# Summing the softmax divisor on four 32-column tiles of TensorE instead of two 64-column tiles (with two smaller edits at the start and the end)

## The chip, the core and the metric

The kernel runs on one core of a Trainium2 chip. The metric is device time in microseconds (us) of one execution. Three runs of the kernel before gave 939.42, 934.87 and 938.68 us, a median of 938.68 us.

## The reference, cut to what matters

```python
# attention: q, k, v are (4, 8, 768, 64), proj is (64, 6)
q_bits = einsum('bhsd,dk->bhsk', q, proj) > 0        # the same for k
mask   = (bucket of q_bits) == (bucket of k_bits)     # bucket = the 6 bits as a number
scores = where(mask, q @ k.T / 8, -1e9)
attn   = exp(scores - max(scores))
attn   = attn / (sum(attn over keys) + 1e-9)
x      = (attn @ v) as (3072, 512)
# feed-forward: w_in is (512, 2048), w_out is (2048, 512)
h  = x @ w_in
g  = h * erf(softplus(h))
out = g @ w_out
```

The change touches the line that divides by the sum over the keys.

## The kernel before, in words

**Attention.** Two heads make a pair: their 64 rows each fill the 128 partitions, and there are 16 pairs. A pair's 768 queries are worked on in two halves of 384, so there are 32 halves, numbered `h`. For each half the 768 keys come as six blocks of 128. `score` (L521) makes a block's scores for both heads on TensorE, `exponential` (L535) turns them into `e` on ScalarE, `sum_keys` (L547) adds the six `e` tiles of 128 keys x 2 heads x 384 queries element by element on VectorE, and `weigh` (L561) multiplies `e` by `v` on TensorE. Once for each pair, `hash_bits` (L358) projects the next pair's q and k.

**The divisor.** `sum_keys` leaves a tile of 128 partitions; the sum over its partitions is done by TensorE. `divisor` (L592) multiplies by a 128x64 matrix of ones, once for each head, so that head 0 lands on PSUM rows 0 to 63 and head 1 on rows 64 to 127, 384 queries each. An f32 product is two matmul instructions here, so a half gives four of them. `keep_divisor` (L604) copies the 128x384 result to SBUF on ScalarE. When both halves of a pair are there, `spread` (L633) writes one row of each head to DRAM with two DMAs on SyncE's queue, `gather` (L637) reads the 1536 numbers back over 128 partitions, `invert` (L645, L648) takes reciprocals on VectorE, `ungather` (L653) and `widen` (L662) bring them back to 64 rows for each head, `normalise` (L670) multiplies on VectorE, and `send` (L676) stores the pair's rows to DRAM. The last pair's share of this is done by `late` inside the feed-forward part.

**The weights.** The host gives the weights as 64-bit floats. `fetch_weights` (L431) loads them in 32 pieces of 512 KB into two buffers; ScalarE and VectorE turn each into f32 (`square_high` to `add_rest`, L445 to L507), between the attention's own work. The first two pieces are loaded on SyncE's queue, behind the second pair's q, k and v; the other 30 on GpSimd's.

**Feed-forward.** 3072 tokens go in six tiles of 512. Both products are done as seven products instead of eight (Winograd's form of Strassen's method): `product` (L1044) makes the seven of the first, `project` (L1184) the seven of the second (M1 to M7), which gather over four steps in seven PSUM banks. After a tile's last step `combine` (L1199, L1215, L1223) adds the banks into the four output blocks on VectorE and stores them. The last step of all uses the order `LAST` (M5 as the last but one, M3 last); M3's block is then added and stored in two halves.

**What sets the order.** Each part lists its operations with an engine, a cost in us, a rank and the operations that it comes after. `arrange` places them greedily in time by these costs and so fixes the order of the instructions on each engine. The costs are only used for that; on the chip each engine runs its list in order and waits for data.

Of the kernel before, what the change touches and what calls it, by code (L numbers as in the profile page):

```python
# [59 lines left out]
ALU = mybir.AluOpType  # L60
# [3 lines left out]
P = 128  # L64
# [16 lines left out]
class Op:  # L81
# [20 lines left out]
    exponential=(3.56, 5.29),  # L102
# [91 lines left out]
def kernel(  # L194
# [206 lines left out]
    def attention():  # L401
        NS = NPAIR * 4
        with (
# [19 lines left out]
            def fetch_weights(n):  # L423
                if n >= len(pieces):
                    return
                queue = nc.sync if n < 2 else nc.gpsimd
                if not WIDE:
                    queue.dma_start(out=pieces[n][0], in_=pieces[n][1])
                else:
                    raws[n] = rawp.tile([P, WP, 2], I32, name="raw", tag="raw")  # L430
                    queue.dma_start(  # L431
                        out=raws[n][:, :, :].rearrange("p c two -> p (c two)"), in_=pieces[n][1]
                    )
# [151 lines left out]

            def divisor(h):

                i, half = divmod(h, 2)
                d = pairs[i]
                z = d["z_ps"] = bank("z_ps")[:, 0:HS]  # L590
                for ab in range(2):
                    nc.tensor.matmul(  # L592
                        out=z[ab * D : ab * D + D, :],
                        lhsT=ones,
                        rhs=d["sum", half][:, ab, :],
                        start=True,
                        stop=True,
                    )
            def keep_divisor(h):
                i, half = divmod(h, 2)  # L600
                d = pairs[i]
                if half == 0:
                    d["z"] = home(i, "z")
                nc.scalar.copy(out=d["z"][:, half * HS : (half + 1) * HS], in_=d.pop("z_ps"))  # L604

            def leave(h):

# [19 lines left out]
            def spread(i):  # L627

                d = pairs[i]
                zd = d["zd"] = dram.tile([2, S], F32, name="zd", tag="zd")  # L630
                d["zc"] = small.tile([P, 2 * S // P], F32, name="zc", tag="zc")
                for ab in range(2):
                    nc.sync.dma_start(out=zd[ab : ab + 1, :], in_=d["z"][ab * D : ab * D + 1, :])  # L633

            def gather(i):
                d = pairs[i]
# [107 lines left out]
            for what, n in order:  # L744
                if what == "score":
                    i = n // 4
                    after = tuple(("weigh_bits", i, ab) for ab in range(2)) + (("copy_bits", i),)
                    for c in range(GC):
                        free = (slots[-3],) if len(slots) >= 3 else ()
                        pe(score, (n, c), 0.82, after + free)  # L750
                        slots.append(("exponential", n, c))
                elif what == "bits":
                    pe(bits_of, (n,), 1.34, (("start_pair", n), slots[-3]))
                    slots.append(("sign_of", n))
                elif what == "divisor":
                    last = 2 * n + 1
                    pe(divisor, (n,), 0.72, (("sum_keys", last, GC - 1), ("keep_divisor", n - 1)))
                else:
                    h = n // 2
                    after = (("exponential", n, GC - 1),)  # L760
                    if n % 2 == 0:
                        after += (("leave", h - 1), ("leave_plain", (h - 1) // 2))
                    pe(weigh, (n,), 2.02, after)
# [21 lines left out]
            for h in range(NH - 1):  # L785
                i = h // 2
                op(
                    keep_divisor,
                    (h,),
                    "ACT",  # L790
                    0.48,
                    (0, 2 * h, -1),
                    (("divisor", h), ("send", i - 1) if i == NPAIR - 1 else ("widen", i - 1)),
                )
# [5 lines left out]
            for i in range(NPAIR):  # L800
# [32 lines left out]
                        )  # L833
                if i == NPAIR - 1:
                    continue
                op(spread, (i,), "SP", 0.8, (0, n, 0), (("keep_divisor", 2 * i + 1),), late=3.0)
                op(gather, (i,), "SP", 0.35, (0, n, 1), (("spread", i),), late=4.5)
                op(invert, (i,), "DVE", 0.4, (0, n + 8, 3), (("gather", i),))
                op(ungather, (i,), "SP", 0.35, (0, n, 2), (("invert", i),), late=3.0)
# [11 lines left out]
            for n in range(len(pieces)):  # L851
                op(
                    fetch_weights,
                    (n,),
                    "SP" if n < 2 else "POOL",
                    1.0,
                    (0, n),
                    (("start_pair", 1), ("fetch_weights", n - 1), ("add_rest", n - 2), ("exponential", max(2 * n - 2, 0), 1)),
                    late=7.0,
                )  # L860
                fetched = ("fetch_weights", n)
                op(square_high, (n,), "ACT", 0.68, (1, n, 0), (fetched, ("mask_bits", n - 1)))
                op(keep_normal, (n,), "ACT", 0.7, (1, n, 1), (("square_high", n),))
                op(move_bits, (n,), "DVE", 1.05, (2, n, 0), (fetched, ("add_rest", n - 1)))
                op(mask_bits, (n,), "DVE", 1.1, (2, n, 1), (("move_bits", n), ("keep_normal", n)), late=1.5)
                op(add_rest, (n,), "DVE", 1.3, (2, n, 2), (("mask_bits", n),))
# [131 lines left out]
    def feed_forward(check, late):  # L998
        again = late is None
        with (  # L1000
# [194 lines left out]
            def combine(t, k):  # L1195

                if k == 0:
# [1 line left out]
                    nc.scalar.copy(out=outs["u"], in_=banks["M1"])  # L1199
                    return  # L1200
                u = outs["u"]
                name, into, one, where, subs = (
                    ("M2", "c", u, (0, 0), (0, 2)),
                    ("M6", "u", u, None, (0, 2)),
                    ("M7", "w", u, None, (0, 2)),
                    ("M4", "c", outs.get("w"), (1, 0), (0, 2)),
                    ("M5", "u", u, None, (0, 2)),
                    ("M5", "w", outs.get("w"), (1, 1), (0, 2)),
                    ("M3", "u", u, (0, 1), (0, 1)),
                    ("M3", "u", u, (0, 1), (1, 2)),  # L1210
                )[k - 1]
                if into == "c" or k == 3:
                    outs[into] = outp.tile([P, 2, TH], F32, name=into, tag=into)
                subs = slice(*subs)
                nc.vector.tensor_tensor(  # L1215
                    out=outs[into][:, subs, :],
                    in0=banks[name][:, subs, :],
                    in1=one[:, subs, :],
                    op=ALU.add,
                )  # L1220
                if where:
                    r0 = t * T + where[0] * TH + subs.start * P
                    nc.sync.dma_start(  # L1223
                        out=out[
                            r0 : r0 + (subs.stop - subs.start) * P,
                            where[1] * TH : (where[1] + 1) * TH,
                        ].rearrange("(s p) d -> p s d", p=P),
                        in_=outs[into][:, subs, :],
                    )

            ops = []
# [2 lines left out]
                ops.append(Op(name, engine, cost, rank, lambda: fn(*args), **more))  # L1234

            ORDER = ("M1", "M2", "M4", "M5", "M6", "M7", "M3")
            LAST = ("M1", "M2", "M4", "M6", "M7", "M5", "M3")
            EMPTIED = dict(M1=0, M2=1, M6=2, M7=3, M4=4, M5=6, M3=8)
            chain = dict(P=None, M=None, X=None)

            def first_ops(p):
# [63 lines left out]
            def between_ops(p, v):  # L1305
# [3 lines left out]
                for k, (fn, engine, cost, after, more) in enumerate(  # L1309
# [8 lines left out]
                    )  # L1318
                ):
                    after += (previous,) if previous else ()  # L1320
                    if again and previous is None:
                        after += tuple(("gate", p - 1, n) for n in range(2))
                    previous = (fn.__name__, p, v)
                    rank = (1, p + PRIORITY[fn.__name__][v], 0)
                    op(previous, engine, cost, rank, fn, me, after=after, **more)
# [48 lines left out]
            def second_ops(p):  # L1374
# [20 lines left out]
                    M7=(S[2],),  # L1395
                    M3=(S[3],),
                )
                for k, name in enumerate(LAST if p == NP - 1 else ORDER):
                    for f in range(4):
                        me = (name, p, f)  # L1400
                        after = needs[name]
# [43 lines left out]
                else:  # L1445
# [9 lines left out]
                        late=5.0,  # L1455
                    )
                if c == NC4 - 1:
                    for k, (name, others) in enumerate(
                        (
                            ("M1", (("combine", t - 1, 8),)),  # L1460
                            ("M2", (0,)),
                            ("M6", (1,)),
                            ("M7", (2,)),
                            ("M4", (3,)),
                            ("M5", (3,)),
                            ("M5", (4, 5)),
                            ("M3", (5,)),
                            ("M3", (7,)),
                        )
                    ):  # L1470
                        after = ((name, p, 1 if k == 7 else 3),) + tuple(
                            ("combine", t, o) if isinstance(o, int) else o for o in others
                        )
                        op(
                            ("combine", t, k),
                            "DVE" if k else "ACT",
                            0.4 if k > 6 else 0.69 if k else 0.58,
                            (0, p, 30 + k),
                            combine,
                            (t, k),  # L1480
# [144 lines left out]
```

## Time and profile before

| what | value |
|---|---|
| runs | 934.87, 938.68, 939.42 us |
| the profiled execution | 939.42 us, of which 937.5 us are the span of the profile |
| TensorE (PE) busy | 920.8 us (98%) |
| VectorE (DVE) busy | 834.6 us (89%) |
| ScalarE (ACT) busy | 776.2 us (83%) |
| DMA read and written | 64.07 MB and 15.93 MB |
| attention | from the start to about 343 us |
| feed-forward | from about 343 us to the end |

PE's busy time counts matmuls whose ends are modelled, so it does not mean that PE is at its peak. PEld is the load of the stationary operand, which may run beside a matmul. "SPq" is SyncE as the issuer of DMAs. In the chain of waits each step is the time from one piece's beginning to that of the next piece that depended on it; it runs from the last instruction back to the first.

### The profile page before, as it was taken

The numbers are of one execution on the slowest core, as the hardware profiler recorded it, in microseconds if no ns is written. First come the engines' busy times: TensorE is split into PE (matmuls) and PEld (weight loads), VectorE is DVE, ScalarE is ACT, GpSimd is POOL, SyncE is SP. The second block draws the span as 40 slices with busy tenths as digits, with TensorE's granted clock in tenths as the row PEclk, the third lists the DMA queues.
The fourth block names the chain that finished last, engine by engine and source line by source line (L and its number), as shares of the span: only waits on it lengthen the run. The fifth ranks groups of instructions, "written<-read, shape, count | busy, mean of one in ns | idle before, by whom it ended". The sixth has DMA issues, their size and how long they took to land.

```text
span 937.5 us, 12887 instructions
## 1 busy us (share of the span) xinstructions
PE 920.8 (98%) x4875; PEld 666.0 (71%) x4875; DVE 834.6 (89%) x1099; ACT 776.2 (83%) x1002; POOL 17.4 (2%) x35
## 2 busy tenths in 40 slices
PE   8999999999999999999999999999999999999996
PEld 3444444444444458888888888888888888888885
DVE  5998999999999987899999989998899789988995
ACT  5888778867888747999997998899989997899891
POOL 0000000000000000000000000000000000000000
PEclk9999999999999999999999999999999999999999
DMA  8355545565664323010222012211221111011211
GB/s 197 97 152 153 132 130 146 136 193 153 170 159 131 97 86 99 15 45 35 68 78 79 34 35 78 79 34 34 79 66 48 34 59 54 34 34 46 68 35 48
DMA packets 59222, 80.91 MB, mean 86 GB/s; under 512 B 33264, under 2 KB 41968, under 8 KB 59152
## 3 DMA queue, kind: packets, MB, share of 16 engines
q1 hardware_dynamic: 54496, 64.08, 23.9%
q0 software_dynamic: 4352, 15.73, 5.5%
q8 instruction: 40, 0.66, 0.3%
q14 instruction: 30, 0.25, 0.1%
q10 hardware_dynamic: 304, 0.20, 0.1%
HBM read 64.07 MB, written 15.93 MB: 85 GB/s over the span
## 4 chain that ended last, share of the span: by engine, by line
PE 88%; DVE 6%; DMA 2%; SPq 1%; issue 1%; ACT 1%; DVEq 0%; ACTq 0%
PE M L1184 30%; PE X L1044 27%; PE st L521 13%; PE av L561 10%; PE M L1044 3%; PE bits L358 2%; PE z_ps L592 2%; DVE sum L547 2%; DMA zd<-z 1%; DMA zc<-zd 1%; SPq L342 0%; PE warm L698 0%; DVE top L481 0%; DVE e L1098 0%; SPq L347 0%
## 5 line engine op out<-in xcount | busy, mean ns | idle before, releaser
L1111 DVE SCALAR_TENSOR_TENSOR e<-w,e 128x1024 f32<-128x1024 f32 x144 | 173.3, 1219 | 6.2 <-ACT w L1107 3.0
L1107 ACT ACTIVATE w<-w,cq 128x1024 f32<-128x1024 f32 x144 | 160.6, 1143 | 1.9
L535 ACT ACTIVATE e<-st 128x768 f32<-128x768 f32 x192 | 149.5, 817 | 13.1 <-PE st L521 12.8
L521 PE MATMUL st<-q,k 64*128 64x384 f32 x768 | 156.8, 486 | 0.0
L1184 PE MATMUL M<-w_out_sb,h 128*128 128x256 f32 x576 | 140.2, 379 | 0.4 <-DVE h L1126 0.4
L547 DVE TENSOR_TENSOR sum<-sum,e 128x768 f32<-128x768 f32 x128 | 122.1, 954 | 8.5 <-ACT e L535 0.6
L561 PE MATMUL av<-e,v 128*64 128x385 f32 (+1 forms) x768 | 129.4, 486 | 0.0
L1044 PE MATMUL X<-x,w_in_sb 128*128 128x256 f32 x512 | 121.1, 379 | 0.0
L1184 PEld LDWEIGHTS M<-w_out_sb,h 128*128 128x128 f32 x576 | 109.2, 190 | 16.0 <-DVE h L1126 1.3
L1044 PEld LDWEIGHTS X<-x,w_in_sb 128*128 128x128 f32 x512 | 97.0, 190 | 13.8 <-ACT h L1062 0.6
L561 PEld LDWEIGHTS av<-e,v 128*64 128x64 f32 x768 | 55.1, 137 | 68.8 <-issue 68.1
L1184 PE MATMUL M<-wt,S 128*128 128x256 f32 x384 | 93.4, 379 | 0.4 <-DVE S L1141 0.4
L521 PEld LDWEIGHTS st<-q,k 64*128 64x128 f32 x768 | 68.8, 189 | 35.1 <-issue 34.9
L1044 PE MATMUL X<-x_sum,w_sum 128*128 128x256 f32 x344 | 81.7, 380 | 1.8 <-ACT h L1062 1.8
L1184 PEld LDWEIGHTS M<-wt,S 128*128 128x128 f32 x384 | 72.9, 190 | 10.7 <-DVE S L1141 0.8
L1044 PEld LDWEIGHTS X<-x_sum,w_sum 128*128 128x128 f32 x344 | 65.0, 190 | 12.0 <-ACT h L1062 3.3
L1062 ACT COPY h<-X 128x512 f32<-128x512 f32 x85 | 49.0, 576 | 22.3 <-PE X L1044 21.4
L521 PE MATMUL st<-qb,kb 64*128 64x384 bf16 x384 | 64.1, 326 | 3.4 <-ACT e L535 2.4
L1088 DVE SCALAR_TENSOR_TENSOR w<-w,e 128x1024 f32<-128x1024 f32 x48 | 58.4, 1220 | 9.7 <-ACT w L1083 9.6
L1126 DVE TENSOR_TENSOR h<-h,e 128x1024 f32<-128x1024 f32 x48 | 57.9, 1220 | 6.1 <-ACT e L1122 5.9
L1102 ACT ACTIVATE w<-e 128x1024 f32<-128x1024 f32 x48 | 50.4, 1050 | 13.3 <-DVE e L1098 13.1
L1098 DVE TENSOR_TENSOR e<-e,w 128x1024 f32<-128x1024 f32 x48 | 57.4, 1217 | 2.6 <-ACT e L1094 2.6
(107 smaller groups left out, 1338.6 us busy)
## 6 DMA issues: line engine op xcount, KB each, us to landing
wt<-wt SPq DMA_DIRECT2D x24, 768.0 KB
raw<-in_w_out_dram POOLq DMA_DIRECT2D x16, 512.0 KB, 3.9
raw<-in_w_in_dram POOLq DMA_DIRECT2D x14, 512.0 KB, 4.0
v<-in_v_dram SPq DMA_DIRECT2D x32, 192.0 KB
xs<-x SPq DMA_DIRECT2D x16, 384.0 KB
q<-in_qkT_dram SPq DMA_DIRECT2D x30, 192.0 KB
k<-in_qkT_dram SPq DMA_DIRECT2D x30, 192.0 KB
r<-rd SPq DMA_DIRECT2D x30, 192.0 KB
```

Of the source, the lines that this page charges most:

```text
L521: nc.tensor.matmul(out=st[:, ab, 0:HS], lhsT=d["k" + src][rows, keys], rhs=d["q" + src][rows, cols], start=(part == 0), stop=(part == 1),)
L535: nc.scalar.activation(out=e[:, :, 0:HS], in_=st[:, :, 0:HS], func=AF.Exp, scale=scale)
L547: nc.vector.tensor_tensor(out=d[key], in0=before, in1=block(n, c)[:, :, 0:HS], op=ALU.add)
L561: nc.tensor.matmul(out=d["av"][rows, 0:w], lhsT=d["v"][:, g * GC + c, rows], rhs=e[:, ab, 0:w], start=(g == 0 and c == 0), stop=(g == 1 an ...
L1044: nc.tensor.matmul(out=d[where][:, u, :], lhsT=a[:, kc, f : f + P], rhs=b[:, kc, :], start=(first and u == 0 and kc == 0), stop=(last and ...
L1088: nc.vector.scalar_tensor_tensor(out=w, in0=w, scalar=-1.0, in1=st[p]["e", v], op0=ALU.add, op1=ALU.subtract)
L1098: nc.vector.tensor_tensor(out=s, in0=s, in1=st[p].pop(("w", v)), op=ALU.subtract)
L1102: nc.scalar.activation(out=z, in_=st[p]["s", v], func=AF.Square)
L1107: nc.scalar.activation(out=q, in_=z, func=AF.Square, bias=cq[:, j : j + 1])
L1111: nc.vector.scalar_tensor_tensor(out=s, in0=st[p].pop(("q", v, j)), scalar=ERF_Q[j][1], in1=s, op0=ALU.add, op1=ALU.mult,)
L1126: nc.vector.tensor_tensor(out=h, in0=h, in1=st[p].pop(("s", v)), op=ALU.mult)
L1184: nc.tensor.matmul(out=banks[name][:, sub, :], lhsT=a[:, u, sub * P : (sub + 1) * P], rhs=b[:, u, :], start=(c == 0 and k == 0), stop=(c = ...
```

## The change

1. `divisor` makes four products instead of two: each of the two heads is cut into two parts of 192 queries, and each product uses 32 columns of ones and lands on 32 PSUM rows of its own. `keep_divisor` copies 128x192 instead of 128x384. `spread` now needs four DMAs for each pair, each of two runs of 192 numbers. The planner's costs follow: 0.42 instead of 0.72 for `divisor`, 0.34 instead of 0.48 for `keep_divisor`, 1.2 instead of 0.8 for `spread`.
2. The first two raw pieces of weights are loaded on GpSimd's queue like the others, and no longer come after the second pair's loads in the plan.
3. `combine` goes back to one order of M1 to M7 for every step, with M5 read into an output tile of its own (`v`), and with M3's block added and stored whole. One more line, for the path that runs only when the scores are out of bounds, loses a condition.

```diff
-                queue = nc.sync if n < 2 else nc.gpsimd
+                queue = nc.gpsimd
...
-                z = d["z_ps"] = bank("z_ps")[:, 0:HS]
-                for ab in range(2):
+                z = d["z_ps"] = bank("z_ps")[:, 0 : HS // 2]
+                for n in range(4):
+                    ab, part = divmod(n, 2)
                     nc.tensor.matmul(
-                        out=z[ab * D : ab * D + D, :],
-                        lhsT=ones,
-                        rhs=d["sum", half][:, ab, :],
+                        out=z[n * QR : (n + 1) * QR, :],
+                        lhsT=ones[:, 0:QR],
+                        rhs=d["sum", half][:, ab, part * HS // 2 : (part + 1) * HS // 2],
...
-                nc.scalar.copy(out=d["z"][:, half * HS : (half + 1) * HS], in_=d.pop("z_ps"))
+                nc.scalar.copy(
+                    out=d["z"][:, half * HS // 2 : (half + 1) * HS // 2], in_=d.pop("z_ps")
+                )
...
-                for ab in range(2):
-                    nc.sync.dma_start(out=zd[ab : ab + 1, :], in_=d["z"][ab * D : ab * D + 1, :])
+                for n in range(4):
+                    ab, part = divmod(n, 2)
+                    nc.sync.dma_start(
+                        out=zd[ab : ab + 1, :].rearrange("a (h l c) -> a h l c", h=2, l=2)[:, :, part],
+                        in_=d["z"][n * QR : n * QR + 1, 0:HS].rearrange("p (h c) -> p h c", h=2),
+                    )
...
-                    pe(divisor, (n,), 0.72, (("sum_keys", last, GC - 1), ("keep_divisor", n - 1)))
+                    pe(divisor, (n,), 0.42, (("sum_keys", last, GC - 1), ("keep_divisor", n - 1)))
...
-                op(spread, (i,), "SP", 0.8, (0, n, 0), (("keep_divisor", 2 * i + 1),), late=3.0)
+                op(spread, (i,), "SP", 1.2, (0, n, 0), (("keep_divisor", 2 * i + 1),), late=3.0)
...
-                    "SP" if n < 2 else "POOL",
+                    "POOL",
...
-                    (("start_pair", 1), ("fetch_weights", n - 1), ("add_rest", n - 2), ("exponential", max(2 * n - 2, 0), 1)),
+                    (("add_rest", n - 2), ("exponential", max(2 * n - 2, 0), 1)),
...
-            LAST = ("M1", "M2", "M4", "M6", "M7", "M5", "M3")
-            EMPTIED = dict(M1=0, M2=1, M6=2, M7=3, M4=4, M5=6, M3=8)
+            EMPTIED = dict(M1=0, M2=1, M6=2, M7=4, M4=5, M5=6, M3=7)
...
-                for k, name in enumerate(LAST if p == NP - 1 else ORDER):
+                for k, name in enumerate(ORDER):
...
-                            ("M7", (2,)),
-                            ("M4", (3,)),
-                            ("M5", (3,)),
-                            ("M5", (4, 5)),
-                            ("M3", (5,)),
-                            ("M3", (7,)),
+                            ("M5", (2,)),
+                            ("M7", (3,)),
+                            ("M4", (4,)),
+                            ("M5", (5,)),
+                            ("M3", (3,)),
```

More of the change, by code (lines that the diff above doesn't have):

```diff
@@ L790, in attention @@
                     "ACT",
-                    0.48,
+                    0.34,
                     (0, 2 * h, -1),
@@ L1201, in combine @@
                 u = outs["u"]
[L1202 to L1210, printed above, removed]
+                name, into, one, where = (
+                    ("M2", "c", u, (0, 0)),
+                    ("M6", "u", u, None),
+                    ("M5", "v", u, None),
+                    ("M7", "u", u, None),
+                    ("M4", "c", u, (1, 0)),
+                    ("M5", "u", u, (1, 1)),
+                    ("M3", "v", outs.get("v"), (0, 1)),
                 )[k - 1]
@@ L1213, in combine @@
                     outs[into] = outp.tile([P, 2, TH], F32, name=into, tag=into)
[L1214 to L1220, printed above, removed]
+                nc.vector.tensor_tensor(out=outs[into], in0=banks[name], in1=one, op=ALU.add)
                 if where:
-                    r0 = t * T + where[0] * TH + subs.start * P
+                    r0 = t * T + where[0] * TH
                     nc.sync.dma_start(
[L1224 to L1228, printed above, removed]
+                        out=out[r0 : r0 + TH, where[1] * TH : (where[1] + 1) * TH].rearrange(
+                            "(s p) d -> p s d", p=P
+                        ),
+                        in_=outs[into],
                     )
@@ L1320, in between_ops @@
                     after += (previous,) if previous else ()
-                    if again and previous is None:
-                        after += tuple(("gate", p - 1, n) for n in range(2))
                     previous = (fn.__name__, p, v)
@@ L1457, in second_ops @@
                 if c == NC4 - 1:
+                    done = {n: (n, p, 3) for n in ORDER}
                     for k, (name, others) in enumerate(
                         (
-                            ("M1", (("combine", t - 1, 8),)),
+                            ("M1", (("combine", t - 1, 6),)),
                             ("M2", (0,)),
                             ("M6", (1,)),
-                            ("M7", (2,)),
-                            ("M4", (3,)),
-                            ("M5", (3,)),
-                            ("M5", (4, 5)),
-                            ("M3", (5,)),
-                            ("M3", (7,)),
+                            ("M5", (2,)),
[3 more added lines that the diff above has]
+                            ("M3", (3,)),
                         )
                     ):
-                        after = ((name, p, 1 if k == 7 else 3),) + tuple(
+                        after = (done[name],) + tuple(
                             ("combine", t, o) if isinstance(o, int) else o for o in others
@@ L1476, in second_ops @@
                             "DVE" if k else "ACT",
-                            0.4 if k > 6 else 0.69 if k else 0.58,
+                            0.69 if k else 0.58,
                             (0, p, 30 + k),
```

## The prediction

> **What bounds the kernel now.** I read the busy shares first, then the chain of waits, then the waits by engine, then SyncE's issues in order of time. The page's first and fourth parts:
>
> ```profile
> PE 920.8 (98%) x4875; PEld 666.0 (71%) x4875; DVE 834.6 (89%) x1099; ACT 776.2 (83%) x1002; POOL 17.4 (2%) x35
> ...
> PE 88%; DVE 6%; DMA 2%; SPq 1%; issue 1%; ACT 1%; DVEq 0%; ACTq 0%
> ```
>
> TensorE is the bound over most of the span, so an edit of its work shows in the time almost fully, but in attention only: by line, the divisor (z_ps, L592) has 2% of the chain. The same chain between 290 and 315 us, with start, length and what:
>
> ```profile
> 289.65 1.44 PE bits L358 x8
> 291.09 0.65 PE z_ps L592 x4
> 291.74 3.88 PE av L561 x24
> 295.62 4.95 PE st L521 x36
> 300.57 0.80 PE z_ps L592 x4
> 301.36 3.87 PE av L561 x24
> ```
>
> Here PE never waits, and a divisor costs 0.65 us behind `bits` and 0.80 us behind scores. `bits`, z_ps and av are of one shape (128x64 stationary); scores are 64x128. Two products of one pass run beside each other: 24 of av take 3.87, or 0.32 for each two. So 0.65 is two passes of 0.32, and 0.80 has 0.15 more for a change of shape. `bits` agrees: four passes make 1.29, and it takes 1.44 behind scores. In the feed-forward part, behind 128x128 products, the last divisor also takes 0.80 (350.34 us).
>
> But PE isn't the only bound. In the stretches of 60 to 210 and 210 to 330 us:
>
> ```profile
> 60.00:210.00 150.00, 146.61 (x964) 68.69 (x962) 139.11 (x212) 116.13 (x207) 7.92 (x15) 1.00 0.58 153
> 210.00:330.00 120.00, 120.00 (x800) 56.70 (x798) 113.45 (x178) 95.16 (x171) 5.80 (x11) 1.00 0.52 139
> ```
>
> The columns are the length, then PE, PEld, DVE, ACT and POOL busy, clock, DMA share, GB/s. PE loses 3.39 us in the first stretch and nothing in the second; VectorE stands at 93% and 95%. In the first stretch the chain goes through VectorE and the divisor's round trip (zd, zc), three times. The waits say why:
>
> ```profile
> DVE zc L645 <- DMA zc<-zd: 6.1, 5, 1.8
> ```
>
> Five of 16 times VectorE stood until the gathered divisors landed (6.1 us in all).
>
> **Part by part.** The sums start from the profiled execution, 939.42 us (937.5 of span and 1.9 around it), which is 0.74 above the median of 938.68.
>
> *PE.* A divisor becomes two passes of four products of 192 queries. If the four run beside each other, as two do now, a pass is 0.16 and the two 0.32 instead of 0.65. But z_ps is then 128x32 between neighbours that are 128x64 or 64x128. No row shows a change from 64 to 32 columns. The nearest are the 0.15 from 64x128 to 128x64 and the same 0.15 from 128x128 to 128x64, where only columns change; I take 0.15. The free lower end is 0. So behind scores: 0.15 + 0.32 + 0.15 (now paid by av) = 0.62 instead of 0.80, -0.18; behind `bits`: 0.62 instead of 0.65, -0.03. By the order of the halves, 17 divisors stand behind scores, 14 behind `bits`, one in the feed-forward part, where both changes exist already (-0.32). Sum: -3.1 - 0.4 - 0.3 = **-3.8 us**. With changes between column counts free it would be 32 x -0.32 = -10.2. If the hardware ran only two of the four beside each other, two passes stay at 0.64 and only the changes are added: 17 x 0.14 + 14 x 0.29 = +6.5.
>
> The Trainium skill speaks against the larger gain: "TensorEngine Tiling (Array Packing)", section Key Properties, says that a change of tiling mode, not a mere change of tile, drains the array, and that page lists 128x64 and 128x32 as different modes. By that rule the sum is the -3.8, without it -10.2; the trace shows the drain for other pairs of modes only (0.15).
>
> The Trainium skill's "TensorE: Matmul & The Clock Gate", section Measured speedup vs the span model, gives 2.38 for three column tiles, not 3. An estimate from that page: four tiles at the same share give 3.17, so 0.40 for 0.32, and PE would gain 2.6 less (-1.2). No run here shows four column tiles.
>
> *ScalarE.* A copy of 384 takes 0.473 and an exponential of 768 takes 0.817, so 192 take about 0.30: 0.17 less for each of 32. ScalarE is busy 116 of 150 us there and rarely ends a wait; cost nothing.
>
> *Spread.* Two DMAs become four on SyncE. Two take 0.64 of issue:
>
> ```profile
> 85.61 1.18 SPq L347 DMA_DIRECT2D v<-in_v_dram  x2
> 86.90 0.64 SPq L633 DMA_DIRECT2D zd<-z  x2
> 90.61 0.35 SPq L637 DMA_DIRECT2D zc<-zd  x1
> 94.55 0.35 SPq L653 DMA_DIRECT2D rd<-zc  x1
> ```
>
> So `gather` is issued 0.64 later, and with it the landing for which `invert` stands on VectorE, in order, with the key sums and the next pair's bits behind it. Where VectorE has no wait (11 of 16) it is hidden; the lower end is 0. The upper end is all five: 3.2 us. PE lost its time in two spots of the first stretch (111 and 196 us), each at the end of a chain through zc; I take 2 x 0.64 = **+1.3**. The smaller copies don't offset it; they make it at most 0.17 less. The last pair's four DMAs lie in the feed-forward part (352 us), their result is needed for the second tile, some 100 us later: nothing.
>
> *First weights.* On GpSimd's queue nothing stands before the two raw loads but the small load of `row` (to 1.9 us), so they go out at about 2 to 3.3 us instead of 9.5 to 10.8. Behind them stands only the third piece, which waits for their buffers until 27 us anyway. They now share the DMA engines with the first pair's second halves:
>
> ```profile
> 4.00:5.00 1.00, 0.94 (x2) 0.20 (x2) 0.59 (x7) 0.00 (x0) 0.00 (x0) 1.00 0.68 186
> 5.00:6.00 1.00, 0.94 (x4) 0.23 (x4) 0.00 (x0) 0.00 (x0) 0.00 (x0) 1.00 0.61 178
> ```
>
> By 6.0 us 800 KB had moved, and the first q and k are 786 KB, so they were there about 2.0 us before PE took the second half (8.03, where it waited for ScalarE). A raw piece lands 4.1 us after issue, so they overlap between 4 and 8 us. Sharing evenly, the 364 KB of these two rows take 2 us more: just the slack. All 1024 KB ahead at 245 GB/s would take 4.2, or 2.2 beyond the slack. No gain is possible, since a ScalarE result sets 8.03 now. Bounds 0 and 2.2; I take **+0.5**, near the even split. SyncE's queue loses 1.24 us of issue before the third pair's loads, which nothing waits for. The pieces' first reader runs at 21.4 us: nothing.
>
> *The end.* M5, not M6, comes after M4 and needs only the first sum: PE's wait of 0.41 at 922.1 us goes. Then three VectorE additions (0.65 each) crowd into the 1.73 us of M3 (+0.2), M3's own is 0.69 instead of a last half of 0.38 (+0.3), and its store 256 KB instead of 128 KB (+0.5 at 250 GB/s): +0.6. Against it, the last issue before took 1.90 us where others took 0.35 to 0.39; without that, -0.9. Between these I take 0.
>
> *The order.* The planner sees a shorter PE and a longer SyncE, and other combine steps. What that does no row shows; the bounds are PE's own idle time, which could go or come again: 3.4 either way in attention, 2.1 in feed-forward (1.03, 0.40 and 0.67 in 400 to 500, 500 to 600 and 360 to 400). The value is 0: most of both parts has no idle PE, and the order within it decides nothing.
>
> Sum: -3.8 + 1.3 + 0.5 = -2.0, so **937.4 us**.
>
> **Rivals.**
>
> *Changing column counts is free* (0.20). For: z_ps to av keeps the rows. Against: the 0.15 at 350.34, where rows are kept too. PE's pair falls from 20.53 (289.65 to 310.18) by 0.64 to 19.89. SyncE's round from one `send` to the next (pair loads, spread, gather, ungather, widen) took 19.41 us at its quickest (251.43 to 270.84); with 0.64 more it is 20.05 and becomes the bound: 15 x 0.16 = 2.4 given back. -10.2 + 2.4 + 0.5 = -7.3: 932.1.
>
> *SyncE's round decides* (0.14). From 82.72 to 232.00 seven rounds took 21.33 each, longer than PE's pair of 20.53, and `spread` starts as soon as the pair loads are issued, so every round would be 0.64 longer: +4.5, +0.5 for the start, less 8 pairs x 0.21 and 0.3 at the last: +3.0, 942.4. Against: later rounds caught up at 19.4.
>
> *Four products aren't four beside each other* (0.16): the change doesn't do what it says. +6.5 + 1.3 + 0.5 = +8.3: 947.7, slower than before. It decides as soon as a pass of four takes over about 0.24 us. For: no row shows four. Against: f32 passes take the same time in one tile of 256 columns (0.216) as two beside each other (0.32 for 384).
>
> **How the numbers follow.** My forecast has 0.50, its own range 935 to 940.5. A measurement of this kernel tells about 0.5% from no change: below 934.0 is faster, over 943.4 slower. Faster: the first rival's 0.17 and 0.03 of my case's edge, 0.20. Slower: the last's 0.15, 0.05 of the second (with the start's upper end) and 0.02 of mine, 0.22. Same: 0.58. The range takes in the first rival and the second with its upper bounds, and stops short of the last: 932 to 945.
>
> **What would show it.** z_ps to av in the chain at 0.47 and av at 4.02 (right), or z_ps near 0.32 and av 3.87 (first rival), or a z_ps group whose passes start 0.32 apart (last). VectorE's wait for zc should rise by 0 to 3 us. `bits` at the start begins its second half near 8.5 us. I'd be wrong by more if the new order put a wait into feed-forward, where PE has no room.

## The result, and the profile after

The changed kernel took 947.57 us, the median of four runs (946.00 to 950.21). The kernel before took 938.22 in the four runs that stand beside them. The ratio is 1.0108, with a 95% interval of 1.0073 to 1.0143. So it is slower by about 9.4 us, where 937.4 and a range of 932 to 945 were forecast. The profiled execution took 946.00 us, of which 944.2 are the span.

The first and fourth parts of the page of after:

```profile
PE 919.1 (97%) x5003; PEld 664.6 (70%) x5003; DVE 837.4 (89%) x1093; ACT 768.7 (81%) x1004; POOL 22.7 (2%) x37
...
PE 78%; DVE 10%; DMA 5%; ACT 4%; issue 2%; SPq 1%; DVEq 0%; ACTq 0%
```

TensorE is busy for 1.7 us less than before, yet the span is 6.7 longer. PE's share of the chain fell from 88% to 78%. VectorE and DMA took up 7 of the 10 points. So something holds PE up. The stretches show where. The columns are again the length, then PE, PEld, DVE, ACT and POOL busy, clock, DMA share and GB/s:

```profile
60.00:210.00 150.00, 142.25 (x982) 65.46 (x982) 134.48 (x206) 106.25 (x197) 9.27 (x14) 0.98 0.57 146
210.00:330.00 120.00, 117.24 (x833) 55.33 (x831) 109.06 (x168) 89.89 (x164) 7.91 (x11) 1.00 0.52 140
360.00:400.00 40.00, 37.98 (x177) 32.29 (x176) 32.45 (x45) 33.65 (x39) 0.00 (x0) 1.00 0.22 75
```

Between 60 and 330 us PE stands idle for 10.5 us, where it was 3.4 before. In the early feed-forward, 360 to 400, it loses another 1.35 (it was busy for 39.33 of these 40 us before). VectorE and ScalarE are less busy as well, so nobody has become a busy bound. It is a wait. The first product of the feed-forward begins at 350.69 instead of 343.17.

In this execution two of TensorE's waits also cost more than their length. It stood from 96.9 to 99.0 us and from 197.0 to 199.7, and soon after each the granted clock is 0.50 for about 3.4 us; over the whole first stretch it is 0.98 in the row above, where the kernel before has 1.00. Four f32 products of the scores (`q,k`) ahead of the second wait and behind it, as start, length and what, with the wait in brackets:

```profile
196.21 0.81 PE L521 MATMUL st<-q,k 64*128 64x384 f32 x4
...
199.74 0.50 PE L521 MATMUL st<-qb,kb 64*128 64x384 bf16 x2 [2.72 <-ACT e L535]
...
200.01 1.51 PE L521 MATMUL st<-q,k 64*128 64x384 f32 x4
```

Half of 3.4 us is 1.7 us for each of the two, an estimate from these rows, and it counts as busy time. It isn't what makes the kernel slow as a whole: e1, below, loses as much with a clock of 1.00 in all three stretches.

One place of the chain of waits of after shows the whole of it (start, length, what; steps under 0.2 us are left out):

```profile
276.27 0.46 PE z_ps L594 x8
276.73 4.05 PE av L561 x24
280.79 0.43 SPq L347
...
281.26 0.54 SPq L347
...
281.90 0.61 SPq L639
...
282.55 0.59 SPq L639
...
283.19 0.54 SPq L639
...
283.77 3.52 DMA zd<-z
...
287.43 1.76 DMA zc<-zd
...
289.56 0.91 DVE sum L547
...
290.56 0.96 DVE sum L547
291.52 0.61 DVE top L481
...
292.16 0.68 ACT keep L445
292.84 0.71 ACT e L535
```

Read it from the top. The divisor is as quick as forecast: z_ps 0.46, av 4.05. Then the chain leaves TensorE and runs through SyncE, which issues the last loads of v (L347) and behind them the DMAs of `spread` (L639). The three of them that lie in the chain take 0.54 to 0.61 us each. Then come the landing in DRAM, the gather, and VectorE, which has stood at `invert` until the gather lands at 289.2. Behind `invert`, in VectorE's order, stand two key sums and a weight's top bits (`top`). ScalarE's `keep` stands for that `top`, an exponential stands behind `keep`, and the next scores on TensorE stand for the exponential. What delays PE is thus neither VectorE's speed nor ScalarE's, but a queue of instructions behind one late landing.

The same in SyncE's issues at 83 us. The columns are start, length and what, and x4 is four DMAs in a row:

```profile
85.52 1.17 SPq L347 DMA_DIRECT2D v<-in_v_dram  x2
86.79 2.42 SPq L639 DMA_DIRECT2D zd<-z  x4
92.86 0.35 SPq L646 DMA_DIRECT2D zc<-zd  x1
95.12 0.35 SPq L662 DMA_DIRECT2D rd<-zc  x1
```

Before, two DMAs took 0.64 here. Now four take 2.42. One DMA of a single run of 768 numbers has a median issue of 248 ns, and one DMA of two runs of 192 numbers has 564 ns. The gather goes out 6.07 us after `spread` begins, instead of 3.71; over 15 pairs the mean is 4.65 instead of 3.36. The waits of the first 350 us on VectorE and on PE, of after (us in all, times, longest):

```profile
DVE zc L654 <- DMA zc<-zd: 10.9, 8, 2.0
...
PE st L521 <- ACT e L535: 10.5, 11, 2.7
```

The same two before:

```profile
DVE zc L645 <- DMA zc<-zd: 4.8, 4, 1.8
...
PE st L521 <- ACT e L535: 2.4, 2, 1.2
```

### The profile page after: what moved, and what is told of

Same layout as the page of the kernel before. It is cut to its first block, busy times and chain, and to the rows that moved or that the text cites. A ratio compares the mean times of both kernels' runs of the same rounds, so it can differ in the third digit from the quotient of the medians.

```text
span 944.2 us, 13127 instructions
## 1 busy us (share of the span) xinstructions
PE 919.1 (97%) x5003; PEld 664.6 (70%) x5003; DVE 837.4 (89%) x1093; ACT 768.7 (81%) x1004; POOL 22.7 (2%) x37
## 4 chain that ended last, share of the span: by engine, by line
PE 78%; DVE 10%; DMA 5%; ACT 4%; issue 2%; SPq 1%; DVEq 0%; ACTq 0%
PE M L1193 30%; PE X L1053 27%; PE st L521 8%; PE av L561 8%; DVE sum L547 3%; PE bits L358 2%; ACT e L535 2%; DMA zd<-z 2%; PE M L1053 2%; DMA zc<-zd 1%; SPq L639 1%; PE z_ps L594 1%; DVE top L481 1%; DMA q<-in_qkT_dram 1%; ACT keep L445 1%
## 5 line engine op out<-in xcount | busy, mean ns | idle before, releaser
L535 ACT ACTIVATE e<-st 128x768 f32<-128x768 f32 x192 | 144.9, 818 | 9.8 <-PE st L521 9.5
L561 PEld LDWEIGHTS av<-e,v 128*64 128x64 f32 x768 | 52.4, 136 | 67.5 <-issue 64.5
L521 PE MATMUL st<-qb,kb 64*128 64x384 bf16 x384 | 63.9, 327 | 10.5 <-ACT e L535 10.5
L618 ACT COPY x<-av 128x384 f32<-128x384 f32 x32 | 15.3, 480 | 61.9 <-PE av L561 40.2
L521 PEld LDWEIGHTS <-kb 64*128 64x128 bf16 x384 | 23.2, 94 | 59.4 <-issue 36.6
```

The lines of the kernel that those rows point to most:

```text
L521: nc.tensor.matmul(out=st[:, ab, 0:HS], lhsT=d["k" + src][rows, keys], rhs=d["q" + src][rows, cols], start=(part == 0), stop=(part == 1),)
L535: nc.scalar.activation(out=e[:, :, 0:HS], in_=st[:, :, 0:HS], func=AF.Exp, scale=scale)
L561: nc.tensor.matmul(out=d["av"][rows, 0:w], lhsT=d["v"][:, g * GC + c, rows], rhs=e[:, ab, 0:w], start=(g == 0 and c == 0), stop=(g == 1 an ...
```

## The experiments

All times are medians, and "before" is the kernel before in the same call. The theories were two: that SyncE's four DMAs and the queue behind `invert` are the loss (the "queue"), and that the order made from the new costs is (the "order").

**1. Which part of the change is it?** `e1_quarters_only` is the kernel before with part 1 alone (all hunks of `divisor`, `keep_divisor`, `spread` and their three costs). `e2_rest_only` is after without part 1. `e8_start_only` is before with part 2 alone.

> The kernel before with part 1 of the change alone (four quarters, shorter copies, four DMAs in spread, the new planner costs); the start and the end stay as before. Theory QUEUE (the four DMAs take 2.4 us of SyncE's issue for each pair instead of 0.64, so SyncE's round from send to send becomes longer than PE's pair): attention ends near 350 us as in the changed kernel, 944 to 949 us in all. Theory ORDER (the new planner costs put the instructions in a worse order): the same 944 to 949. Theory REST (the raw loads on GpSimd's queue and the end are to blame): 933 to 937, by the 3.8 us that PE saves.

> The changed kernel without part 1 (two halves, two DMAs in spread, the old costs), so only the edits of the start and the end. QUEUE and ORDER: 936 to 941, as before. REST: 945 to 951.

> The kernel before, and only the first two raw pieces go on GpSimd's queue, with the changed conditions in the plan. If the first pair's loads pay for it as the profiles of the changed kernel show (the second half of bits begins at 9.5 to 9.8 us instead of 8.0): 938.5 to 940 against a before of 937.2. If that delay is made up later: 936.5 to 938.

Measured: e1 948.05 against 937.15, ratio 1.0125 [1.0097, 1.0153]; e2 938.42 against 937.15, 1.0017 [1.0004, 1.0029]; e8 939.69 against 936.79, 1.0026 [1.0014, 1.0038]. So the loss is part 1: +10.9 from it and +1.3 from parts 2 and 3 together make +12.2, which the interval of after takes in (6.8 to 13.4). Part 2 alone costs 2.4 by the ratio. VectorE's waits for zc in e1 are 13.0 us in ten, PE's for the exponential 12.4.

**2. The four DMAs or the order?** The kernel before with one of the two alone. `e3_four_dmas_only` keeps the halves and the old costs and cuts `spread` into four:

```diff
-                for ab in range(2):
-                    nc.sync.dma_start(out=zd[ab : ab + 1, :], in_=d["z"][ab * D : ab * D + 1, :])
+                for n in range(4):
+                    ab, part = divmod(n, 2)
+                    nc.sync.dma_start(
+                        out=zd[ab : ab + 1, :].rearrange("a (h l c) -> a h l c", h=2, l=2)[:, :, part],
+                        in_=d["z"][ab * D : ab * D + 1, :].rearrange("p (h l c) -> p h l c", h=2, l=2)[:, :, part],
+                    )
```

`e5_costs_only` changes only the three costs (0.72 to 0.42, 0.48 to 0.34, 0.8 to 1.2). `e10_new_costs_four_dmas` does both, still in halves.

> The kernel before, and only spread is cut into four DMAs of two runs of 192 numbers each, from the rows where the kernel before has them; planner costs, order and TensorE's work as before. QUEUE: spread takes about 2.4 us of issue, the quickest round of SyncE grows from 19.4 to 21.2 us, above PE's pair of 20.5: 12 rounds by 0.65 are 8 us, so 943 to 950, and more than twice 6.1 us of VectorE waiting for zc. ORDER: the order is that of before: 937 to 941.

> The kernel before with only the three planner costs of the change (0.42, 0.34, 1.2); all instructions are those of before, their order may differ. ORDER: 940 to 945, with more of VectorE's and TensorE's waiting than before. QUEUE: 936 to 939, since no instruction takes longer than before.

> No quarters: two products of 384 as before, the new planner costs, and four DMAs of two runs in spread. If the new order is what makes the four DMAs dear: 944 to 949. If it takes PE's shorter pair as well: 939 to 942.5, as with the old costs (941.0).

Measured: e3 941.01 against 937.15, 1.0048 [1.0030, 1.0066]; e5 936.72 against 936.79, 0.9998 [0.9984, 1.0011]; e10 945.63 against 937.81, 1.0088 [1.0070, 1.0107]. The order alone costs nothing, the DMAs alone 3.9 us, less than expected, and both 7.8. They aren't two terms that add up. With the halves, the new order is harmless as long as two DMAs bring the result, and it doubles the price of four.

**3. The quarters with fewer DMAs.** A head's two rows can go in one DMA, so that two serve a pair:

```diff
-                for n in range(4):
-                    ab, part = divmod(n, 2)
+                for ab in range(2):
                     nc.sync.dma_start(
-                        out=zd[ab : ab + 1, :].rearrange("a (h l c) -> a h l c", h=2, l=2)[:, :, part],
-                        in_=d["z"][n * QR : n * QR + 1, 0:HS].rearrange("p (h c) -> p h c", h=2),
+                        out=zd[ab : ab + 1, :].rearrange("a (h l c) -> (a l) h c", h=2, l=2),
+                        in_=d["z"][ab * D : ab * D + D : QR, 0:HS].rearrange("p (h c) -> p h c", h=2),
                     )
```

`e4_after_two_dmas` is after with this; `e9_quarters_new_costs_two_dmas` is e1 with this; `e6_quarters_old_costs` is e1 with the old costs and four DMAs; `e7_quarters_old_costs_two_dmas` has the old costs and two.

> The changed kernel, and spread uses two DMAs, each with both rows of a head; planner costs and so the order as in the changed kernel. QUEUE: issue falls to some 1.2 us, the round to 20.0 or less, under PE's pair of 20.3: 934 to 940. ORDER: 945 to 949, since the order is the changed kernel's.

> Part 1 with its four DMAs, but with the planner costs of before (0.72, 0.48, 0.8), so in the order of before. ORDER: the cost of the four DMAs as measured alone (3.9) and PE's saving (3.8) about cancel: 936 to 939. QUEUE: with a shorter PE pair SyncE's round bites more, as in the changed kernel: 943 to 948.

> As the last, and with two DMAs in spread, each with both rows of a head. ORDER: 933 to 936, PE's saving of 3.8 less little. QUEUE: 938 to 942, as the changed kernel with two DMAs (941.9).

> Part 1 with the new planner costs and two DMAs instead of four; it completes the table of costs (old, new) by DMAs (two, four) on the quarters. If the order by the new costs is bad for the quarters by itself: 939 to 943 (the changed kernel with two DMAs had 941.9, of which the start and the end are 1.3). If it is only bad together with the long issue of four DMAs: 933 to 936, as with the old costs.

Measured: e4 941.86 against 937.15, 1.0054 [1.0038, 1.0071]; e6 938.82 against 936.79, 1.0038 [1.0019, 1.0056]; e7 933.40 against 936.79, 0.9958 [0.9943, 0.9974]; e9 938.63 against 937.81, 1.0014 [1.0002, 1.0027]. The two DMAs issue for 1.1 us together, still 0.5 more than before. e4 and e9 fell between the ranges of their two theories, e9 next to the range for an order that is bad for the quarters by itself. All eight corners, each as its median's difference to its own "before" in us:

| products | costs | two DMAs | four DMAs |
|---|---|---|---|
| halves | old | 0 | +3.9 (e3) |
| halves | new | -0.1 (e5) | +7.8 (e10) |
| quarters | old | **-3.4** (e7) | +2.0 (e6) |
| quarters | new | +0.8 (e9) | +10.9 (e1) |

From the left column to the right it is +3.9, +7.9, +5.4 and +10.1: four DMAs cost something in every row, about twice as much under the new costs. From halves to quarters it is -3.4 and -1.9 under the old costs, +0.9 and +3.1 under the new. So TensorE's saving is there, and is lost where the new costs set the order, even with two DMAs (4.2 us lie between e7 and e9). e7 is faster than both kernels. Its stretches:

```profile
60.00:210.00 150.00, 147.21 (x1036) 67.49 (x1034) 141.81 (x216) 114.92 (x208) 7.92 (x15) 1.00 0.58 158
210.00:330.00 120.00, 120.00 (x854) 55.22 (x850) 113.35 (x178) 95.27 (x173) 5.81 (x11) 1.00 0.49 135
360.00:400.00 40.00, 39.32 (x183) 34.23 (x182) 36.43 (x41) 39.08 (x43) 0.00 (x0) 1.00 0.15 46
```

PE is as full as in the kernel before (146.61, 120.00 and 39.33), and the feed-forward's first product begins at 338.01 instead of 343.17.

**4. Is it the planner's picture of the round trip?** The planner was told 1.2 us for a `spread` that takes 2.42, so it may place `invert` too early. `e11_spread_cost_2p4` is e1 with the true cost. `e13_part1_three_x` is e1 with a third buffer for `x`, since ScalarE's copies of x also wait for stores (z and r, which shared two buffers, have one each for it), `e14_two_dmas_three_x` is e7 with it, and `e15_spread_2p4_three_x` has both changes. `e16_late_invert_three_x` is e13 with only `gather`'s lateness in the plan raised.

The cost in e11 and e15, the buffer in e13 to e16, and the lateness in e16:

```diff
-                op(spread, (i,), "SP", 1.2, (0, n, 0), (("keep_divisor", 2 * i + 1),), late=3.0)
+                op(spread, (i,), "SP", 2.4, (0, n, 0), (("keep_divisor", 2 * i + 1),), late=3.0)
...
-                    return xst.tile([P, S], F32, name=what, tag="x" if what == "x" else "z")
+                    return xst.tile(
+                        [P, HS if what == "z" else S], F32, name=what, tag=what, bufs=3 if what == "x" else 1
+                    )
...
-                op(gather, (i,), "SP", 0.35, (0, n, 1), (("spread", i),), late=4.5)
+                op(gather, (i,), "SP", 0.35, (0, n, 1), (("spread", i),), late=6.5)
```

> Part 1 as in the changed kernel, with four DMAs, and the planner told that spread takes 2.4 us of SyncE (the measured issue) instead of 1.2, so that invert is placed two key sums later on VectorE. If the loss is VectorE standing at invert for a divisor that comes late: 937 to 943 and less than half of the 13.0 us of waits for zc of part 1 alone. If the place of invert is not what matters: 946 to 950.

> Part 1 as in the changed kernel (quarters, four DMAs, new costs), and x has three SBUF buffers instead of two; room is made by giving z 384 columns and a buffer of its own, r another, as they are used one after the other anyway. If ScalarE's copy of x, waiting for the store of the x two pairs before, is what holds the exponentials and so TensorE: 936 to 942 and hardly any of 14.3 us of waits for xs left. If VectorE at invert is: 945 to 949, with zc near 13 us.

> Quarters, old planner costs, two DMAs (933.4 to 934), with the three x buffers. If x buffers hold it: 930.5 to 932.5, since about 2.5 us of TensorE's waiting in attention are left there. If not: 933 to 934.5.

> Part 1 with four DMAs, the planner told 2.4 us for spread, and three x buffers (e11 and e13 together). If VectorE's wait at invert and ScalarE's wait for an x buffer are the two ends of one squeeze: 936 to 942, with neither wait above some 3 us. If a third thing in this order costs the time: 946 to 952.

> Part 1 with four DMAs and three x buffers, spread's cost left at 1.2, and the planner told that gather lands after 6.5 us instead of 4.5, which also puts invert two key sums later. Squeeze: 936 to 942. A third thing: 946 to 952.

Measured: e11 952.08 against 937.81, 1.0154 [1.0134, 1.0173]; e13 947.04 against 937.81, 1.0094 [1.0078, 1.0111]; e14 935.32 against 937.81, 0.9972 [0.9963, 0.9982]; e15 937.09 against 936.38, 1.0001 [0.9987, 1.0015]; e16 943.15 against 936.38, 1.0053 [1.0036, 1.0071].

e11 went against the expectation, and its waits (first 350 us) say why:

```profile
ACT x L618 <- DMA xs<-x: 38.3, 8, 7.2
ACT x L618 <- PE st L521: 20.3, 4, 5.4
ACT x L618 <- PE av L561: 14.4, 15, 2.8
PE st L521 <- ACT e L535: 12.4, 12, 2.7
```

No wait for zc is left in this stretch, so `invert` does come later. The plan has changed in another place as well: `spread` now stands directly behind `send` in 14 of 15 pairs, where in e1 it stands behind the loads of v in 12 of 15. So e11, e15 and e16 don't test the place of `invert` alone. With the late `invert`, `normalise` and `send` come later too, the two buffers of x come free later, and ScalarE's copy of x stands until the store (xs) has gone, with the exponentials behind it. PE's own wait for the exponential is just what it was in e1, and 3.8 us in seven waits for ScalarE's copy of the divisor (z), which e1 doesn't have, come on top. In e13, with the third buffer and the early `invert`, it is the other way round:

```profile
DVE zc L656 <- DMA zc<-zd: 13.0, 10, 2.4
PE st L521 <- ACT e L535: 12.3, 12, 1.9
```

In e15, with both, the waits for zc and xs are gone in these 350 us, none of PE's for the exponential is in the list, and so is the loss, with all four DMAs of 0.56 us still there. That doesn't give the -3.4 of e7: VectorE now waits for r, the reciprocals brought back to 64 rows (8.1 us in four), PE waits for the copy z (4.0 us in seven, none in e7), and PE has 147.96 of 150 in the first stretch, but 117.87 of 120 in the second and 37.78 of 40 between 360 and 400, where VectorE still stands 4.4 us for the last pair's zc. e16 moves `invert` without the true cost and still loses 6.8 by medians, 5.0 by the ratio, between the ranges of its two theories. Its waits for zc and xs are gone in these 350 us as well; those for r are 9.4 us in seven, and PE's for z 5.8 in nine. So the waits for zc and xs are not the whole of the loss, and what e16 loses by isn't shown. And e14 shows that the third buffer brings nothing of its own where the round trip is short (0.9972 beside e7's 0.9958).

**5. The end.** `e12_quarters_two_dmas_end` is e7 with part 3.

> The quarters with two DMAs and the old planner costs (933.4), with the end of the changed kernel (part 3) and the start of before. Part 3 takes 1.3 off by the difference of the runs with start and end and with the start alone: 931 to 933.5. If part 3 gains nothing: 933 to 934.5.

Measured: 934.24 against 937.81, 0.9966 [0.9953, 0.9980], beside 0.9958 for e7. The runs don't resolve part 3: each against its own before, by medians, e2 stands 1.6 below e8, and e12 0.2 below e7. Nor do the traces. The stretch from the first X product to the end of the span is 564.7 us in after and in e2 and 566.9 in before, but 566.1 in both e12 and e7. Much of this is the issue of the last store, which took 0.37 us in after and e2, 1.89 in e12 and 1.90 in before.

## Why the prediction was wrong

*TensorE, -3.8: right.* z_ps and av together fell from 4.67 to 4.48 us behind scores (-0.18 forecast) and from 4.53 to 4.49 behind `bits` (-0.03 forecast). They show 0.46 and 4.02 to 4.05, as the last part of the forecast named them. e7 gained 3.4 by medians, 2.4 to 5.3 by its interval. So a pass of four 32-column products does run as four beside each other (two passes take 0.46, where two by two they would take 0.64 alone), and the rival "four products aren't four beside each other" falls, though its time (947.7) is the measured one. The other rival, free changes of column counts, falls with av at 4.02.

*Spread, +1.3: this is the step that failed.* The text priced the two new DMAs at 0.32 each, from DMAs of one unbroken run. The new ones have two runs of 192 each. The nearest row was then another of the same view, the pair loads of v, at 1.18 for two. All four got dearer, not only the two that were added: +1.78 instead of +0.64. The bound of 3.2 was five waits at 0.64; five at 1.78 are 8.9. With 1.78 the text's own two spots come to 3.6, near the 3.9 that e3 shows for the four DMAs in the old order; the rest came with the new order. The second error was to let the number of waits stand. A round trip that is longer by 1.3 in the mean made ten of them in e1, and eight in after, in the first 350 us, where before had four. The text's own sign was 0 to 3 us more of VectorE's waits for zc; it was 6.1 more in after. In e1 PE's idle time grew by 9.1 between 60 and 330 us and by 1.4 between 360 and 400; by the medians the loss is 14.3 (the 10.9, and the 3.4 that e7 saves). Of these the table gives 10.1 to four DMAs instead of two under the new costs (e1 and e9) and 4.2 to the new costs with two (e9 and e7). The profiled execution of e1 took 945.86, 2.2 below its median, so the trace shows somewhat less than the runs.

*The order, 0 (3.4 either way): right alone, wrong together.* e5 shows 0. But the same costs doubled the price of the four DMAs (e3 and e10), and on the quarters they cost 4.2 even with two. The text treated the edits as terms of a sum. The likely reason that they aren't is that both draw on the same slack, the time between `spread` and `invert` in VectorE's order; the table shows that they don't add, not why.

*The rival "SyncE's round decides" came nearest in its mechanism*, at 0.14. Ten rounds from one `send` to the next took 216.5 us in after (82.72 to 299.18), 21.65 each, and 207.8 before (82.72 to 290.55). PE's pair takes 20.33 (213.13 to 233.46), as forecast. The rival was priced with 0.64 and seven rounds, and so came to +3.0. Whether SyncE's round sets the pace, or is itself stretched by the waits inside it, isn't shown.

*The first weights, +0.5 (0 to 2.2): too little.* e8 gives +2.4 [1.3, 3.6]. That is about the upper bound (all of the raw bytes ahead), not near the even split. Between 4 and 8 us after moved 333, 289, 343 and 325 GB/s where before moved 186, 178, 241 and 245, and yet the wanted q came late:

```profile
9.51 0.83 PE L358 MATMUL bits<-q,proj_sb 128*64 128x384 f32 x2 [1.71 <-DMA q<-in_qkT_dram]
```

Before, this product began at 8.03, and in e8 at 10.70.

*The last pair's four DMAs, "nothing": wrong.* The result is needed 100 us later, but VectorE stands for it in order, whoever needs it. In 360 to 400 us of after:

```profile
DVE zc L654 <- DMA zc<-zd: 3.7, 1, 3.7
```

The feed-forward's own additions are behind it, and PE loses 1.35. On the halves neither the DMAs nor the order does this alone: PE is busy for 39.33 of these 40 us in e3 and in e5. On the quarters each does it in part (38.93 in e6, 38.60 in e9, 37.94 with both in e1).

*The change of mode and the four tiles.* Av behind z_ps went from 3.87 to 4.02, so the change from 32 to 64 columns costs 0.15. The Trainium skill's "TensorEngine Tiling (Array Packing)", section Key Properties, says that a change of mode drains the array; this agrees with it. The skill's "TensorE: Matmul & The Clock Gate", section Measured speedup vs the span model, has 2.38 for three column tiles, from which an estimate was 0.40 for the two passes. z_ps takes 0.46; if 0.15 of it is the change of mode, 0.31 are left, which is the full share of four (0.32), not the 0.40.

**What stays open:** which of the three costs makes the order tight wasn't tried one by one, nor was `spread` on another engine's queue. Part 3's worth is not resolved. Why e15 doesn't reach e7, and why e16 loses 5.0 us with neither wait left in the first 350, is read from waits alone, not shown by an experiment. Nor was the earlier `spread` of e11, e15 and e16 parted from the later `invert`.

## What to carry to other kernels

Price a DMA by its shape, from a row of the nearest shape, not by its bytes: here, an edit that was to save 3.8 us on the busiest engine (and gave 3.4 in e7) split 6 KB into pieces that cost 1.78 us more of issue for each pair. Where engines run their lists in order, ask what stands behind the instruction that waits for a longer round trip, and whether another edit has used up the same slack; two edits that are each cheap alone can cost twice their sum. And a wait that is moved (a later `invert`) has to be followed to the next thing that it makes late, as here to a buffer.

## What the runs showed of the hardware

A DMA from two partitions at once (two rows of two runs, e4 and e7) has a median issue of 0.54 us (0.51 at the least), no more than one from a single row of two runs (0.56), so that two of them do the work of four. The number of runs alone doesn't set the price: the gather over 128 partitions issues in 0.35.

At the start, a matmul pass of 384 columns in f32 takes 0.84 to 0.90 us and later 0.49, while the profile gives the granted clock as 1.00 in before, after and e1. In e4, after a wait of 2.3 us, four f32 products of the scores take 1.49 instead of 0.81 with the clock given as 0.50; in before the same four take 1.49 at 9.9 us with it given as 1.00. The first fast product begins at 12.8 us in the execution of before, at 9.5 in after (which then still stands behind its late q and k) and at 8.0 in e1, and the second pair's `bits` begin at 18.62, 18.56 and 16.43. So up to 2.2 us of a difference between two single executions can come from there, which is why small terms were judged by runs and not by two profiles.

A wait of over 2 us on TensorE can be followed by a half clock: after waits of 2.1 and 2.7 us (after) and of 2.27 us (e11, at 154 us) the granted clock is 0.50 for about 3.4 us. It isn't always: e11 has a wait of 2.68 us at 109 us, and e10 one of 2.07 at 195 us, with the clock at 1.00 behind them.
